# Block sums spread by DMA, a third value buffer, an earlier v load, and two more x tiles transposed by DMA in a sparse-attention and expert-mixture kernel

## The chip, the cores and the metric

The kernel runs on one core of one Trainium2 chip. The metric is device time in microseconds (us). Before the change the median of 6 runs was 668.28 us (667.62 to 671.56).

## The reference

Two stages follow each other. The first is attention over 4 batches of 8 heads, 768 positions and 64 channels. Each query sees the keys less than 16 positions away, and 24 block summaries: the maximum of each block of 32 keys, and the mean of the 32 values. The second sends each of the 3072 rows of x (512 wide) through 8 experts and adds their outputs with weights P, which come from a gate and 8 rounds of row and column normalisation.

```python
k_sum = k.reshape(B, H, nb, block, D).max(axis=3)        # block = 32, nb = 24
v_sum = v.reshape(B, H, nb, block, D).mean(axis=3)
mask_l = np.abs(pos[:, None] - pos[None, :]) < window    # window = 16
scores_s = scale * np.einsum('bhsd,bhnd->bhsn', q, k_sum) + np.log(block)
...                                                      # one softmax over near keys and summaries
x = attn_out.transpose(0, 2, 1, 3).reshape(B * S, H * D)
P = np.exp(logits)                                       # logits = x @ w_gate, less the maximum
for _ in range(8):
    P /= P.sum(1, keepdims=True) + 1e-09
    P /= P.sum(0, keepdims=True) + 1e-09
    P *= N / E
for e in range(E):
    out += P[:, e:e + 1] * (np.maximum(x @ w1[e], 0.0) @ w2[e])
```

## The kernel before, in words

The heads are worked on in 16 pairs (two heads fill the 128 partitions), four pairs to a batch. Pairs 0 to 3 go in halves of 384 positions and have code of their own; the change concerns pairs 4 to 15. For such a pair:

- POOL issues the loads of k, q and v from HBM (`load_qk` L268, `load_v` L285), which are cast to bf16 on the way. k and q are transposed, by TensorE for pairs 4 to 11 (`tr`, L301, tile `tkq`) and by DMA transposes issued on SP for pairs 12 to 15 (`tr_dma`, L328).
- `key_max` takes block maxima of k on VectorE, and `key_max_split` (L339) lays those of the two heads into columns 0 to 63 of `ksT`.
- `block_sums` (L355, tile `vs`) sums v over blocks with 6 matmuls. `block_out` scales the sums into chunk 0 of `V_e` (L361) and copies that chunk to the other five on VectorE (L365). `V_e` holds, for each of the 6 chunks of 128 positions, 64 rows of summaries and 64 rows with the 16 positions next to the chunk on either side. These neighbour rows are copied from v by four small DMAs (`near_values`, L375 and L377), issued on SP for pairs 4 to 11 and on POOL after that. There are NE = 2 buffers of `V_e`.
- `scores` (L345, tile `sg`) multiplies keys and near queries; a head has 64 channels, so these matmuls use 64 rows of the array. ScalarE takes the exponential (L406), and VectorE masks it (L410) and lays the edges out (L418, L422).
- `summaries_2` (L459, tile `ss`) multiplies the block maxima with the queries: two matmuls of 64 columns, one for each half of the positions, into the two halves of the partitions. ScalarE takes the exponential (L470).
- `values` (tile `av`) multiplies weights and values: 6 matmuls on the chunk itself (L433) and 3 with `V_e` (L439), for each half. `normalize` divides (L540, L541).
- `to_xT` transposes the result with 6 matmuls (L548, tile `tx`) and `x_out` copies it out on ScalarE or VectorE; for pairs 12, 13 and 14 a DMA transpose on SP does this (`x_dma`, L558, from X_BY_DMA = 12 on).

Between these units TensorE does expert 0: `hps` (L209, x times w1) and `yps` (L214, hidden times w2), and the gate (`lp`, L568) once for each batch. Experts 1 to 7 follow (L762, L813) with a scheme that saves multiplications by sums formed on VectorE, and with the sums into `out_acc` done by VectorE and by DMAs that add.

The order on every engine is fixed when the program is built. A planner (`Plan.order`) holds units with an engine, a cost, dependences, a priority and a lag, and places the unit that can start first; the costs in `load_pair`, `pair_start` and `pair_whole` decide the order, not the times on the chip. All engines work off their queues in order, so a unit that waits holds up what stands behind it. On POOL stand the loads of a pair, then the next pair's; before batch 1 the order is k and q of pair 4, w2 of expert 0, the constants of two `V_e` buffers (L694 to L697) and two edge buffers (L690), v of pair 4, then pairs 5 and up. On SP stand the neighbour copies of the pairs, and the DMA transposes.

Of the kernel before, what the change touches and what calls it, by code (L numbers as in the profile page):

```python
# [10 lines left out]
BF16 = mybir.dt.bfloat16  # L11
# [117 lines left out]
def kernel(  # L129
# [10 lines left out]
    nc = tc.nc  # L140

    B, H, S, D = q.shape
    G = S // 128
# [6 lines left out]
    NP = (B * H) // 2  # L150
    PB = H // 2
    SCALE = 1.0 / float(D) ** 0.5
    W = 16
# [4 lines left out]
    VD = D + 1  # L158
    NEH = 3
    BY_DMA = 12  # L160
    X_BY_DMA = 12
    WHOLE = 12
    FILL = {"v0": 1, "S0": 1, "s0": 2, "s1": 1, "s2": 1}

# [53 lines left out]
    NQ = 6  # L218
    NB = PB
    NE = 2  # L220
    NS = 1
    NA = 3
    stage = ExitStack()
    with tc.manual_schedule():
# [12 lines left out]
        kT = [attn.tile([128, S], BF16, name=f"kT{i}") for i in range(NB)]  # L237

        ks = [attn.tile([128, 1, 32], BF16, name=f"ks{i}") for i in range(NB)]
        ksT = [attn.tile([128, 128], BF16, name=f"ksT{i}") for i in range(NB)]  # L240
        v_x = [attn.tile([128, 2, G, VD], BF16, name=f"vx{i}") for i in range(NQ)]

        E_h = [attn.tile([128, 2, HG + 1, PADL], BF16, name=f"Eh{i}") for i in range(NEH)]
        V_s = [attn.tile([128, 2 * VD], BF16, name=f"Vs{i}") for i in range(PB)]

        E_e = [attn.tile([128, G, 128], BF16, name=f"Ee{i}") for i in range(NE)]
        V_e = [attn.tile([128, G, 2 * VD], BF16, name=f"Ve{i}") for i in range(NE)]

        BLK = 512
        NPAIR = N // (2 * BLK)  # L250
# [85 lines left out]

        def key_max_split(i):
            r = i % NB
            nc.vector.tensor_tensor(out=ksT[r][:, 0:64].rearrange("p (j n) -> p j n", j=2),  # L339
                                    in0=ks[r][:].to_broadcast([128, 2, 32]),  # L340
                                    in1=own[:].to_broadcast([128, 2, 32]), op=ALU.mult)

# [14 lines left out]

        def block_out(i):
            vs = at.pop(("vs", i))[0:64, :].rearrange("p (j d) -> p j d", j=2)
            dst = V_s[i][0:64, :] if i < PB else V_e[i % NE][0:64, 0, :]  # L360
            nc.vector.tensor_tensor(out=dst.rearrange("p (j x) -> p j x", j=2)[:, :, 0:D], in0=vs,  # L361
                                    in1=own_n[:].to_broadcast([64, 2, D]), op=ALU.mult)
            if i >= PB:
                ve = V_e[i % NE]
                nc.vector.tensor_copy(out=ve[0:64, 1:G, :],  # L365
                                      in_=ve[0:64, 0:1, :].to_broadcast([64, G - 1, 2 * VD]))


        def near_values(i):

            sv, ve = v_x[i % NQ], V_e[i % NE]
            eng = nc.sync if i < BY_DMA else nc.gpsimd
            for j in range(2):
                c0, q0 = VD * j, 64 + 32 * j
                eng.dma_start(out=ve[q0 + W:q0 + 2 * W, 1:G, c0:c0 + VD],  # L375
                              in_=sv[128 - W:128, j, 0:G - 1, :])
                eng.dma_start(out=ve[q0:q0 + W, 0:G - 1, c0:c0 + VD],  # L377
                              in_=sv[0:W, j, 1:G, :])
# [46 lines left out]
                                        op=ALU.mult)  # L425

        def values(i, h):
            sv, ee, ve, em = v_x[i % NQ], E_e[i % NE], V_e[i % NE], at["em", i]
            av = at["av", i, h] = bank("a", "av")
            for cc in range(HG):  # L430
                c, o = HG * h + cc, cc * 2 * VD
                for j in range(2):
                    nc.tensor.matmul(av[:, o + j * VD:o + (j + 1) * VD],  # L433
                                     lhsT=em[:, j, c, :], rhs=sv[:, j, c, :],
                                     start=(cc == 0 and j == 0), stop=False,
                                     skip_group_check=True)
            for cc in range(HG):
                c, o = HG * h + cc, cc * 2 * VD
                nc.tensor.matmul(av[:, o:o + 2 * VD], lhsT=ee[:, c, :], rhs=ve[:, c, :],  # L439
                                 start=False, stop=True, skip_group_check=True)  # L440

        def summaries(i, h, tag):
            r = i % NB
            ss, rhs = bank(tag, "ss"), qT[r][:, W + h * HS:W + (h + 1) * HS]
            wait_busy("s", i, h, ss)
            at["ss", i, h] = ss
            if i < PB and not h:
                for j in range(2):
                    p = slice(64 * j, 64 * j + 64)
                    nc.tensor.matmul(ss[32 * j:32 * j + 32, 0:HS], lhsT=ks[r][p, 0, :], rhs=rhs[p],  # L450
                                     start=True, stop=True)
                return
            nc.tensor.matmul(ss[:, 0:HS], lhsT=ksT[r][:], rhs=rhs, start=True, stop=True)

        def summaries_2(i):
            r, ss = i % NB, bank("a", "ss")
            for h in range(2):
                at["ss", i, h] = ss[64 * h:64 * h + 64]
                nc.tensor.matmul(ss[64 * h:64 * h + 64, 0:HS], lhsT=ksT[r][:, 0:64],  # L459
                                 rhs=qT[r][:, W + h * HS:W + (h + 1) * HS], start=True, stop=True)  # L460

        def summary_exp(i, h):
            if i < PB:
# [187 lines left out]
        def constants():  # L651
# [8 lines left out]
            for t in ks:  # L660
                nc.vector.memset(t[:, 0, 24:32], 0.0)
            for t in ksT:
                nc.vector.memset(t[:, 64:128], 0.0)
# [201 lines left out]
        def load_pair(i, parts="kqv"):  # L865
            old = i - NQ
            for c in parts:
                if c == "v":
                    load(("v", i), lambda: load_v(i), 1.05, 1.85,
                         [U.get(("A", old, 1)), U.get(("near", old))])  # L870
                elif i < PB and c in "qr":
                    h = "qr".index(c)
                    load(("q", i, h), lambda h=h: load_qk(i, 1, h), 0.65, 0.65)
                else:
                    z = "kq".index(c)
                    load((c, i), lambda z=z: load_qk(i, z), 0.75 if i < PB else 1.65,
                         1.2 if i < PB else 1.55, [U.get(("tr", old, z)), U.get(("tr", old, 2))])

        def pair_start(i, prio):
            o = i - NB  # L880
# [20 lines left out]
            U["vs", i] = add("PE", 0.4, lambda: block_sums(i),  # L901
                             [U["v", i]] + ([U.get(("A", i - NE, 1)), U["vc", i % NE]] if i >= PB else []), prio + 0.01, opens=[buf])
            sc = add("DVE", 0.25, lambda: summary_constants(i), [], prio - 1.0) if 0 < i < PB else None
            U["Vs", i] = add("DVE", 0.28 if i < PB else 0.7, lambda: block_out(i), [U["vs", i], sc],
                             prio + 0.01, uses=[buf])

        def pair_half(i, h, prio):
# [33 lines left out]

        def pair_whole(i, prio):
            U["near", i] = add("SP" if i < BY_DMA else "POOL", 2.4 if i < BY_DMA else 3.0, lambda: near_values(i),
                               [U["v", i], U.get(("A", i - NE, 1)), U["vc", i % NE]], prio, lag=3.5)
            x1 = []
            deps = [U["kT", i, 0], U["kT", i, 1], U.get(("ed", i - 2))]
            bufs = [Buffer("s")] + (2 * [None] if i < WHOLE else [Buffer("a"), Buffer("a")])
# [12 lines left out]
            for h in range(2):  # L960
# [5 lines left out]
            U["ss", i, 0] = U["ss", i, 1] = add("PE", 0.22, lambda: summaries_2(i),  # L966
                                                [U["km", i], U["kT", i, 1], U.get(("A", i - NE, 1))], prio, opens=[buf])
# [124 lines left out]
        def transposed():  # L1092
# [6 lines left out]
            ve = V_e[(NP - 1) % NE]  # L1099
# [4 lines left out]
        last[0] = add("POOL", 0.3, transposed, [last[0], U["near", NP - 1]] + [U["kT", NP - 1, z] for z in range(2)]  # L1104
                      + [U["x", i] for i in range(X_BY_DMA, NP - 1)])
        load("w1n", lambda: load_w1(1), 0.85, 5.0)
        load("w2n", lambda: load_w2(1), 0.85, 5.0)
# [209 lines left out]
```

## Time and profile before

| what | value |
|---|---|
| median of 6 runs | 668.28 us (667.62 to 671.56) |
| the profiled execution, its own time | 671.9 us |
| its span, first to last instruction | 670.2 us |
| mean granted TensorE clock | 0.997 |
| packets under 512 B | 77920 of 112542 |
| median time to landing: k, q, v loads | 5.7, 5.5, 6.2 us |
| w (a whole weight), neighbour copies from SP, from POOL | 10.5, 5.2, 2.1 us |
| DMA transposes of k, q, x | 4.8, 4.0, 3.3 us |

The profile is of one execution. Its page gives the busy time of each engine, with TensorE's matmuls as PE and its weight loads as PEld, then the span in 40 slices of 16.8 us in tenths. A matmul's duration is its latency: several overlap, and what one costs the queue is the distance from its start to the start of the next. A wait line reads: engine, tile and line, what it waited for, microseconds in total, how often, the longest. A timeline line reads: start, microseconds, engine, line, operation, output and inputs, the part of the array in rows and columns, shape, how many. A line of the chain that ended last has start, duration and what ran. All lines of code are those of the kernel before.

### The profile page before, as it was taken

The numbers are of one execution on the slowest core, as the hardware profiler recorded it, in microseconds if no ns is written. First come the engines' busy times: TensorE is split into PE (matmuls) and PEld (weight loads), VectorE is DVE, ScalarE is ACT, GpSimd is POOL, SyncE is SP. The second block draws the span as 40 slices with busy tenths as digits, with TensorE's granted clock in tenths as the row PEclk, the third lists the DMA queues.
The fourth block names the chain that finished last, engine by engine and source line by source line (L and its number), as shares of the span: only waits on it lengthen the run. The fifth ranks groups of instructions, "written<-read, shape, count | busy, mean of one in ns | idle before, by whom it ended". The sixth has DMA issues, their size and how long they took to land.

```text
span 670.2 us, 13245 instructions
## 1 busy us (share of the span) xinstructions
PE 660.1 (98%) x5132; PEld 434.8 (65%) x5132; DVE 546.1 (81%) x1027; ACT 415.8 (62%) x776; POOL 198.2 (30%) x256
## 2 busy tenths in 40 slices
PE   9979999999999999999999999999999999999996
PEld 5646665555676666666666666666666666666665
DVE  7859877798989787788779886888778877988776
ACT  6757876565886666656565556656655656556652
POOL 8899522100031221222132222222222113222123
PEclk9989999999999999999999999999999999999999
DMA  9999971610754738374654656473847465334656
GB/s 164 172 144 145 120 97 30 118 21 1 126 95 80 126 62 127 64 128 78 95 95 69 121 86 104 78 126 53 126 76 123 78 100 95 63 63 111 157 134 198
DMA packets 112542, 67.89 MB, mean 101 GB/s; under 512 B 77920, under 2 KB 90464, under 8 KB 112480
## 3 DMA queue, kind: packets, MB, share of 16 engines
q0 software_dynamic: 94800, 57.46, 64.4%
q1 hardware_dynamic: 17152, 9.58, 5.8%
q8 instruction: 40, 0.66, 0.4%
q14 instruction: 22, 0.18, 0.1%
q10 hardware_dynamic: 528, 0.02, 0.0%
HBM read 52.45 MB, written 6.29 MB: 88 GB/s over the span
## 4 chain that ended last, share of the span: by engine, by line
PE 93%; DMA 3%; POOL 2%; SPq 0%; issue 0%; DVE 0%; ACT 0%; POOLq 0%; DVEq 0%
PE yps L813 22%; PE pA L762 22%; PE pY L813 16%; PE pQ L762 11%; PE yps L214 6%; PE hps L209 6%; PE pR L762 5%; DMA w<-in_moe_w_dram 1%; DMA vx<-in_v_dram 1%; DMA Ve<-vx 1%; PE sg L345 1%; PE av L433 1%; PE av L439 1%; PE tkq L301 1%; PE vs L355 1%; PE ss L459 0%
## 5 line engine op out<-in xcount | busy, mean ns | idle before, releaser
L813 PEld LDWEIGHTS <-h 128*128 128x128 f16 x2352 | 229.8, 98 | 89.5 <-issue 1.0
L841 POOL DMA_DIRECT2D out_acc<-y x120 | 101.4, 886 | 372.9 <-ACT y L837 108.8
L837 ACT ACTIVATE y<-pY,P_sb 128x256 f32<-128x256 f32 x168 | 79.9, 476 | 124.1 <-PE pY L813 122.3
L828 DVE SCALAR_TENSOR_TENSOR out_acc<-yps,P_sb,out_acc 128x512 f32<-128x512 f32 x128 | 95.2, 744 | 29.4 <-PE yps L813 29.4
L796 DVE TENSOR_TENSOR h<-h 128x1024 f16<-128x1024 f16 x168 | 109.1, 684 | 1.4
L813 PE MATMUL pY<-w,h 128*128 128x256 f16 x672 | 100.0, 273 | 0.6 <-ACT y L837 0.6
L813 PE MATMUL yps<-w2sum,h 128*128 128x256 f16 x672 | 98.4, 273 | 0.0
L762 PE MATMUL pA<-xT,w 128*128 128x512 f16 x336 | 98.4, 380 | 0.0
L813 PE MATMUL yps<-w,h 128*128 128x256 f16 x672 | 93.2, 273 | 0.0
L828 DVE SCALAR_TENSOR_TENSOR out_acc<-pY,P_sb,out_acc 128x512 f32<-128x512 f32 x84 | 62.9, 748 | 31.6 <-PE pY L813 30.1
L762 PEld LDWEIGHTS <-w 128*128 128x128 f16 x672 | 65.7, 98 | 31.6 <-issue 0.2
L762 PEld LDWEIGHTS <-w1sum 128*128 128x128 f16 x504 | 49.3, 98 | 44.4
L784 DVE CUSTOM_DVE_ANT_0 h<-pQ,snap 128x512 f16<-128x512 f32 x84 | 57.6, 686 | 6.1 <-ACT snap L205 3.6
L784 DVE CUSTOM_DVE_ANT_0 h<-pA,snap 128x512 f16<-128x512 f32 x84 | 57.4, 683 | 5.5 <-PE pA L762 5.2
L200 ACT ACTIVATE h<-pA 128x512 f16<-128x512 f32 x84 | 50.6, 603 | 13.3 <-PE pA L762 13.1
L200 ACT ACTIVATE h<-pR 128x512 f16<-128x512 f32 x84 | 50.1, 596 | 8.6 <-PE pR L762 8.1
L205 ACT COPY pR<-pA 128x512 f32<-128x512 f32 x83 | 47.4, 571 | 6.9 <-PE pA L762 6.0
L813 PE MATMUL pY<-w2sum,h 128*128 128x256 f16 x336 | 50.4, 273 | 0.0
L762 PE MATMUL pQ<-xsum,w1sum 128*128 128x512 f16 x168 | 50.0, 380 | 0.0
L762 PE MATMUL pA<-xsum,w1sum 128*128 128x512 f16 x168 | 50.0, 380 | 0.0
L762 PE MATMUL pQ<-xT,w1sum 128*128 128x512 f16 x168 | 50.0, 379 | 0.0
L762 PE MATMUL pA<-xsum,w 128*128 128x512 f16 x168 | 50.0, 379 | 0.0
(150 smaller groups left out, 854.1 us busy)
## 6 DMA issues: line engine op xcount, KB each, us to landing
out_acc<-y POOLq DMA_DIRECT2D x120, 256.0 KB, 3.4
w<-in_moe_w_dram POOLq DMA_DIRECT2D x15, 1024.0 KB, 10.5
out_dram<-out_acc SPq DMA_DIRECT2D x24, 256.0 KB, 2.4
qst<-in_q_dram POOLq DMA_DIRECT2D x32, 96.0 KB, 5.5
vx<-in_v_dram POOLq DMA_DIRECT2D x15, 192.0 KB, 6.2
kst<-in_k_dram POOLq DMA_DIRECT2D x24, 96.0 KB, 5.7
w<-in_moe_w_dram POOLq DMA_DIRECT2D x4, 256.0 KB, 7.4
kst<-in_k_dram POOLq DMA_DIRECT2D x3, 192.0 KB, 4.5
```

The costliest lines, as they stand in the source:

```text
L200: nc.scalar.activation(out=out, in_=in_, func=AF.Relu, bias=0.0, scale=1.0)
L205: (nc.scalar.copy if eng == "ACT" else nc.vector.tensor_copy)(out=out, in_=in_)
L209: nc.tensor.matmul(hp[:, 0:n], lhsT=w1s[e][:, dk, f * 128:(f + 1) * 128], rhs=xT[:, dk, t0:t0 + n], start=(dk == 0), stop=(dk == KD - 1))
L214: nc.tensor.matmul(yp[:, d], lhsT=h[:, f, c * 128:(c + 1) * 128], rhs=w2s[e][:, f, d], start=(f == 0), stop=(f == KF - 1))
L301: nc.tensor.transpose(t[:, g * 128:(g + 1) * 128], st[:, g, :, :].rearrange("p j d -> p (j d)"), ident)
L762: nc.tensor.matmul(dst[:], lhsT=lhsT, rhs=rhs, start=first and k == 0, stop=k == HK - 1, skip_group_check=True)
L784: nc.vector._custom_dve(dve_ops.TENSOR_ADD_SAT, out=ring(e, p, q)[:, q % 2, blk, :], in0=at[src, e, p, q][:], in1=at.pop(("snap", n, e, p, ...
L796: nc.vector.tensor_tensor(out=h[:, :, out_, :], in0=h[:, :, a, :], in1=h[:, :, b, :], op=op)
L813: nc.tensor.matmul(dst[:, d], lhsT=lhsT, rhs=rhs, start=f == 0 and n in (1, 5, 2), stop=f == HF - 1, skip_group_check=True)
L828: nc.vector.scalar_tensor_tensor(out=o, in0=y, scalar=scalar, in1=o, op0=ALU.mult, op1=ALU.add)
L837: nc.scalar.activation(out=at[key][:, d], in_=src, func=AF.Copy, bias=0.0, scale=P_sb[:, t, e:e + 1])
L841: nc.gpsimd.dma_start(out=o, in_=at.pop(("y", e, p, c, key))[:], accum_op=ALU.add)
```

## The change

- The copy of the block sums to chunks 1 to 5 leaves VectorE. `spread_sums` does it with one DMA that reads chunk 0 five times; it is issued on SP for pairs 4 to 11 and on POOL for 12 to 15, and the values of the pair wait for it.
- `V_e` gets three buffers (NV = 3), with one more set of constants on POOL.
- v of pair 4 is loaded ahead of w2 of expert 0.
- The planner's costs of loads and its lags of the DMAs on SP are changed, and so the order on all engines.
- `ksT` becomes 192 columns wide, zeros on both sides of the keys. The two summary matmuls then take 128 columns each and add into the same bank: the first has the keys in its first 64 columns, the second in its last.
- X_BY_DMA goes from 12 to 9: the results of pairs 9 and 10 are transposed by DMA too (pair 11 is not, as pair 15 is not).

```diff
-    X_BY_DMA = 12
+    X_BY_DMA = 9
...
+    NV = 3
...
-        ksT = [attn.tile([128, 128], BF16, name=f"ksT{i}") for i in range(NB)]
+        ksT = [attn.tile([128, 192], BF16, name=f"ksT{i}") for i in range(NB)]
...
-        V_e = [attn.tile([128, G, 2 * VD], BF16, name=f"Ve{i}") for i in range(NE)]
+        V_e = [attn.tile([128, G, 2 * VD], BF16, name=f"Ve{i}") for i in range(NV)]
...
-            if i >= PB:
-                ve = V_e[i % NE]
-                nc.vector.tensor_copy(out=ve[0:64, 1:G, :],
-                                      in_=ve[0:64, 0:1, :].to_broadcast([64, G - 1, 2 * VD]))
...
+        def spread_sums(i):
+
+            ve = V_e[i % NV]
+            (nc.sync if i < BY_DMA else nc.gpsimd).dma_start(
+                out=ve[0:64, 1:G, :], in_=ve[0:64, 0:1, :].to_broadcast([64, G - 1, 2 * VD]))
...
-                nc.tensor.matmul(ss[64 * h:64 * h + 64, 0:HS], lhsT=ksT[r][:, 0:64],
-                                 rhs=qT[r][:, W + h * HS:W + (h + 1) * HS], start=True, stop=True)
+                nc.tensor.matmul(ss[:, 0:HS], lhsT=ksT[r][:, 64 - 64 * h:192 - 64 * h],
+                                 rhs=qT[r][:, W + h * HS:W + (h + 1) * HS], start=h == 0, stop=h == 1)
...
-                    load(("v", i), lambda: load_v(i), 1.05, 1.85,
+                    load(("v", i), lambda: load_v(i), 1.05, 1.85 if i < PB else 1.6,
...
-                         1.2 if i < PB else 1.55, [U.get(("tr", old, z)), U.get(("tr", old, 2))])
+                         1.2 if i < PB else 1.4, [U.get(("tr", old, z)), U.get(("tr", old, 2))])
...
-                               [U["v", i], U.get(("A", i - NE, 1)), U["vc", i % NE]], prio, lag=3.5)
+                               [U["v", i], U.get(("A", i - NV, 1)), U["vc", i % NV]], prio, lag=5.0 if i < BY_DMA else 3.5)
+            U["sp", i] = add("SP" if i < BY_DMA else "POOL", 0.62 if i < BY_DMA else 0.9, lambda: spread_sums(i), [U["Vs", i]],
+                             prio, lag=5.0 if i < BY_DMA else 3.5)
...
-                                   [U["mk", i, h], U["ed", i], U["sx", i, h], U["Vs", i], U["near", i]],
+                                   [U["mk", i, h], U["ed", i], U["sx", i, h], U["sp", i], U["near", i]],
...
-        load_pair(PB, "kq")
-        load("w2", lambda: load_w2(0), 0.85, 5.0)
+        load_pair(PB, "kqv")
+        load("w2", lambda: load_w2(0), 0.85, 4.0)
+        for n in range(NV):
+            U["vc", n] = last[0] = add("POOL", 1.2, lambda n=n: value_constants(n), [last[0]])
         for n in range(NE):
-            U["vc", n] = last[0] = add("POOL", 1.2, lambda n=n: value_constants(n), [last[0]])
             U["ec", n] = last[0] = add("POOL", 0.7, lambda n=n: edge_constants(n), [last[0]])
...
-            load_pair(i, "v" if i == PB else "kqv")
+            load_pair(i, "" if i == PB else "kqv")
```

More of the change, by code (lines that the diff above doesn't have):

```diff
@@ L338, in key_max_split @@
             r = i % NB
-            nc.vector.tensor_tensor(out=ksT[r][:, 0:64].rearrange("p (j n) -> p j n", j=2),
+            nc.vector.tensor_tensor(out=ksT[r][:, 64:128].rearrange("p (j n) -> p j n", j=2),
                                     in0=ks[r][:].to_broadcast([128, 2, 32]),
@@ L359, in block_out @@
             vs = at.pop(("vs", i))[0:64, :].rearrange("p (j d) -> p j d", j=2)
-            dst = V_s[i][0:64, :] if i < PB else V_e[i % NE][0:64, 0, :]
+            dst = V_s[i][0:64, :] if i < PB else V_e[i % NV][0:64, 0, :]
             nc.vector.tensor_tensor(out=dst.rearrange("p (j x) -> p j x", j=2)[:, :, 0:D], in0=vs,
                                     in1=own_n[:].to_broadcast([64, 2, D]), op=ALU.mult)
-            if i >= PB:
-                ve = V_e[i % NE]
-                nc.vector.tensor_copy(out=ve[0:64, 1:G, :],
-                                      in_=ve[0:64, 0:1, :].to_broadcast([64, G - 1, 2 * VD]))
+        def spread_sums(i):
+            ve = V_e[i % NV]
+            (nc.sync if i < BY_DMA else nc.gpsimd).dma_start(
+                out=ve[0:64, 1:G, :], in_=ve[0:64, 0:1, :].to_broadcast([64, G - 1, 2 * VD]))
         def near_values(i):
-            sv, ve = v_x[i % NQ], V_e[i % NE]
+            sv, ve = v_x[i % NQ], V_e[i % NV]
             eng = nc.sync if i < BY_DMA else nc.gpsimd
@@ L427, in values @@
         def values(i, h):
-            sv, ee, ve, em = v_x[i % NQ], E_e[i % NE], V_e[i % NE], at["em", i]
+            sv, ee, ve, em = v_x[i % NQ], E_e[i % NE], V_e[i % NV], at["em", i]
             av = at["av", i, h] = bank("a", "av")
@@ L452, in summaries @@
                 return
-            nc.tensor.matmul(ss[:, 0:HS], lhsT=ksT[r][:], rhs=rhs, start=True, stop=True)
+            nc.tensor.matmul(ss[:, 0:HS], lhsT=ksT[r][:, 64:192], rhs=rhs, start=True, stop=True)
         def summaries_2(i):
@@ L662, in constants @@
             for t in ksT:
-                nc.vector.memset(t[:, 64:128], 0.0)
+                nc.vector.memset(t[:], 0.0)
             for t, n in ((own, 64), (own_n, 32)):
@@ L901, in pair_start @@
             U["vs", i] = add("PE", 0.4, lambda: block_sums(i),
-                             [U["v", i]] + ([U.get(("A", i - NE, 1)), U["vc", i % NE]] if i >= PB else []), prio + 0.01, opens=[buf])
+                             [U["v", i]] + ([U.get(("A", i - NV, 1)), U["vc", i % NV]] if i >= PB else []), prio + 0.01, opens=[buf])
             sc = add("DVE", 0.25, lambda: summary_constants(i), [], prio - 1.0) if 0 < i < PB else None
-            U["Vs", i] = add("DVE", 0.28 if i < PB else 0.7, lambda: block_out(i), [U["vs", i], sc],
+            U["Vs", i] = add("DVE", 0.28, lambda: block_out(i), [U["vs", i], sc],
                              prio + 0.01, uses=[buf])
@@ L965, in pair_whole @@
             buf = Buffer("a")
-            U["ss", i, 0] = U["ss", i, 1] = add("PE", 0.22, lambda: summaries_2(i),
+            U["ss", i, 0] = U["ss", i, 1] = add("PE", 0.33, lambda: summaries_2(i),
                                                 [U["km", i], U["kT", i, 1], U.get(("A", i - NE, 1))], prio, opens=[buf])
@@ L1098, in transposed @@
                 nc.gpsimd.tensor_copy(out=warm[:, 4:5], in_=xT[0:32, PB - 2, (B - 1) * S:(B - 1) * S + 1])
-            ve = V_e[(NP - 1) % NE]
+            ve = V_e[(NP - 1) % NV]
             for j in range(2):
@@ L1102, in transposed @@
                                       in_=ve[64 + 32 * j:96 + 32 * j, G - 2, VD * j:VD * j + 1])
-        last[0] = add("POOL", 0.3, transposed, [last[0], U["near", NP - 1]] + [U["kT", NP - 1, z] for z in range(2)]
+        last[0] = add("POOL", 0.3, transposed, [last[0], U["near", NP - 1], U["sp", NP - 1]] + [U["kT", NP - 1, z] for z in range(2)]
                       + [U["x", i] for i in range(X_BY_DMA, NP - 1)])
```

## The prediction

> **What bounds the kernel now.** I read the page first, then who waited for whom on TensorE over the whole span, then the chain that ended last around the one wait found there, the stretches in tens of microseconds, and last TensorE's timeline. The page:
>
> ```profile
> span 670.2 us, 13245 instructions
> ## 1 busy us (share of the span) xinstructions
> PE 660.1 (98%) x5132; PEld 434.8 (65%) x5132; DVE 546.1 (81%) x1027; ACT 415.8 (62%) x776; POOL 198.2 (30%) x256
> ...
> PEclk9989999999999999999999999999999999999999
> ```
>
> TensorE (PE) is busy 98% of the span, and one slice of its clock (the third, 33 to 50 us) is not full. The waits of TensorE over the whole span:
>
> ```profile
> PE av L439 <- DMA Ve<-vx: 3.5, 1, 3.5
> PE idle L611 <- DVE zeros L630: 1.3, 1, 1.3
> PE pY L813 <- ACT y L837: 0.6, 1, 0.6
> ```
>
> Everything after that one wait is TensorE-bound: what TensorE saves or loses in attention moves the end by as much, and work taken off VectorE is worth nothing in itself. The wait belongs to pair 4, the first pair of batch 1; the chain leads to it:
>
> ```profile
> 22.94 0.88 POOL w L196
> ...
> 27.88 7.01 DMA vx<-in_v_dram
> ...
> 34.98 0.76 SPq L375
> ...
> 35.80 1.44 SPq L377
> ...
> 37.92 6.59 DMA Ve<-vx
> ```
>
> v of pair 4 is issued at 27.88 behind w2 (22.94), lands at 34.89, the fourth neighbour copy goes out at 37.92 and lands at 44.51; TensorE stood from 41.1. The stretches show what follows (columns: PE busy, clock, DMA share, GB/s):
>
> ```profile
> 30.00:40.00 10.00, 10.00 (x138) 1.00 2.17 155
> 40.00:50.00 10.00, 6.46 (x61) 0.83 2.21 140
> 50.00:60.00 10.00, 10.00 (x117) 1.00 2.32 145
> ```
>
> The granted clock was 0.83 there: 0.17 x 10 = 1.7 us more. The stall costs 3.5 + 1.7 = **5.2 us** of this execution.
>
> **The change, part by part.**
>
> *v of pair 4 ahead of w2.* Its load is issued at about 22.9, five microseconds earlier, so it lands near 29 and the neighbour copies (2.5 to 3.5 us of issue on SP, 4.5 median and 6.7 at most to landing in the rows of Ve) near 38 to 39. The changed order puts TensorE at that pair's values at about 41.0: its block sums stand where w2's first matmul stood (32.80), and between them and L439's successor are 20 yps at 0.216, 24 lp at 0.025, 27 transposes and block-sum matmuls at 0.056, 2 summary matmuls at 0.163, one score group 0.40, the values of pair 3 0.84 and 6 av at 0.03: 8.2 us. So the 5.2 us go. Next late is w2. TensorE's timeline shows it was just in time:
>
> ```profile
> 32.43 0.51 PE L548 MATMUL tx<-ident_x,xs 128*128 128x128 f16 x6
> 32.80 1.02 PE L214 MATMUL yps<-w,h 128*128 128x512 f16 x4
> ```
>
> w2 is issued at 22.91 and its row has 9.8 us to landing: 32.76, against a start at 32.80. One v load ahead of it in the same saturated queue (DMA share above 2 in the stretches) costs between 1.3 (the steady distance from a q landing to the v landing behind it) and 2.1 (v of pair 4 behind w2). The block sums moved ahead give 0.34 back. TensorE then waits 1.0 to 1.7 for w2; I take 1.2. The nearest row for what an idle of that length does to the clock is the 3.5 us stall (-1.7 more); a third as long, I take nothing, and keep 1.7 as the end. In the Trainium skill, "TensorE: Matmul & The Clock Gate" (Part 1) puts the fall to half rate after an idle window of about 3.4 us; the 3.5 us row agrees, and by the page this wait would cost no clock.
>
> *Loads behind it.* The changed order also brings block sums forward: those of pair 9 now stand 21.9 us of TensorE work behind those of pair 4 (32 hps at 0.163, 24 yps, 24 lp, 81 short ones at 0.056, 54 av, 6 score groups, 6 summary matmuls, pair 3's values), at 54.7, plus the w2 wait: 55.9. In the trace before v of pair 9 is issued at 50.44; with the row's 6.2 us it lands at 56.6, which harmed nobody, because its block sums ran at 71.04. The third buffer's constants put 1.33 us more (23.86 to 25.19 is one set) on POOL ahead of these loads, which POOL issues without a break (4.25 us a pair). So v of pair 9 lands at 56.6 to 58.0 and TensorE waits 0.7 to 2.1 more, partly already at pairs 6 and 7; I take 1.0.
>
> *Spread by DMA.* Removes 12 VectorE copies of 0.483 = 5.8 us; no wait of TensorE named VectorE after 48 us, so this is worth 0. Added: 12 issues of about 0.6 on SP or 0.52 on POOL, and a landing of 1.7 to 6.7 us where the copy was done in 0.5. What hides it is the distance from a pair's block sums to its values: for pair 4 8.2 us plus the w2 wait against 0.3 + 0.6 + 4.5 to 6.7, more for later pairs (pair 5: 9.8). Cost 0; a latency beyond 9 us would uncover it, one for one, first at pair 4. Its bytes: 64 x 5 pieces of 260 B, as many pieces as the four neighbour copies together. By pieces that is 320 / 1536 of a v load's 1.3 us, 0.3 of the saturated queue a pair; the other end is a whole v load, 1.3. I take 0.3, the nearest in pieces and size, inside the 1.0 above. The wait on SP stands ahead of the next pair's neighbour copies, whose v lands later anyway.
>
> *Three value buffers* free neighbour copies one pair earlier; those waited on SP, no TensorE wait named them after pair 4: 0.
>
> *Full-width summary scores.* The rows, all at full clock:
>
> ```profile
> 92.92 0.34 PE L439 MATMUL av<-Ve,Ee 128*128 128x130 bf16 x3
> 93.10 0.34 PE L433 MATMUL av<-vx,em 128*128 128x65 bf16 x6
> 93.28 0.34 PE L439 MATMUL av<-Ve,Ee 128*128 128x130 bf16 x3
> 93.54 0.35 PE L459 MATMUL ss<-qT,ksT 128*64 128x384 bf16 x2
> 93.83 1.47 PE L209 MATMUL hps<-xT,w 128*128 128x384 f16 x8
> 95.14 0.51 PE L355 MATMUL vs<-vx,m_blk 128*128 128x128 bf16 x6
> ```
>
> Three av matmuls take 0.18 to the next full-width one but 0.26 to the summary pair, the pair 0.29 until the next starts: 0.37, of which two halves side by side need only 0.16. Full width costs twice 0.164 (hps x8: 1.31) = 0.33 and no change of shape. Eight of the 12 pairs stand behind full-width work and cost 0.37, four behind scores and cost 0.29 (the scores' own way out is paid either way): 4.1 us before, 12 x 0.33 = 3.9 after: **-0.2**. The Trainium skill speaks against this edit: "TensorEngine Tiling (Array Packing)", Theoretical Speedup, gives half-wide tiles up to twice the rate, by which full width would add 12 x 0.16 = 1.9 us; its Key Properties say too that a change of mode drains the engine, and the row of 93.54 prices that above the gain.
>
> *x of pairs 9 and 10 by DMA.* Removes 12 transposes at 0.056 = **-0.7** from TensorE, and two copies (0.8 ScalarE or 0.56 VectorE), off the path. Adds two transposes on SP (1.21 of issue, 3.3 to landing). Behind each on SP's queue stand transposes of k and q for pairs 13 to 15, which in the trace were issued 10 us and more ahead of use. Cost 0; uncovered, one for one.
>
> Sum on this execution: 671.9 - 5.2 - 0.7 - 0.2 + 1.2 + 1.0 = 668.0, a gain of 3.9. Profiled, it took 3.6 more than the median of 668.28. From 48 us on TensorE is full either way, so most of these 3.6 must lie in the loads before it: part of the stall or its slow clock is probably missing from the runs timed, and then part of the new waits too. The gain on the median lies between 1.4 (the stall worth 1.6, new waits 1.1) and 3.9; I take 2.5: **665.8**.
>
> **Rivals.**
> 1. *Nothing new waits*, w2 and the v loads landing sooner than in this execution: 668.28 - 2.5 - 2.2 = 663.6. For it: the median below the profile. Against: w2's margin of 0.04 us.
> 2. *The stall only moves*: the queue sets the pace, and w2 and the v loads cost what the neighbour copies cost. What stays is 0.9 for the matmuls: 667.4. For it: DMA share above 2 until 76 us.
> 3. *Slower*: the spread's 260-byte pieces slow the loads to 5.5 us a pair (4.2 + 1.3). v of pair 5, issued at 32.12 and landed at 39.7, then comes at 41.0, v of pair 9 at 41.0 + 4 x 5.5 = 63.0, 8.3 behind TensorE's 54.7, with one stretch long enough for the clock (1.7): 10.0 against 6.1 taken away, 3.9 slower, 672.2. It decides from a pace of 4.5 (with the slow clock) to 5.0 (without). Against: those pieces take a fifth of a load's number.
> 4. *The change doesn't do what it says*: pair 4 still waits, on its spread in place of its neighbours. That needs 9 us of latency; the longest row is 6.7. Counted in 3.
>
> **How the numbers follow.** Forecast 0.48 at 665.8 (a fifth of it within 0.3% of the median), nothing new waits 0.18, stall only moves 0.23, slower 0.11. About 0.3%, 2.0 us, is what a measurement of this kernel tells from no change: faster 0.48 x 0.8 + 0.18 = 0.56, same 0.33, slower 0.11. The range runs from 663.0 (rival 1 with the loads' lower ends) to 669.5, leaving out most of rival 3 and a little at the bottom.
>
> **What would show it.** Right: no wait at the values of pair 4, a clock of 1.00 from 40 to 50 us; a wait of about 1.2 us of the first yps for w2; small waits of block sums for v at pairs 6 to 9; summary matmuls 128 x 128, 0.33 a pair; attention ending 3 to 5 us earlier in the trace. Wrong: the clock falling again, values waiting for Ve from Ve, block sums waiting over 3 us, or a wait after 130 us, where I expect TensorE to stay full.

## The result, and the profile after

The change made the kernel slower: 672.93 us median of 24 runs (670.63 to 675.89) against 668.84 of 48 runs of the kernel before beside them (666.57 to 673.74), a ratio of 1.0061 with a 95% interval of 1.0047 to 1.0074. The forecast was 665.8, the range 663.0 to 669.5. The profiled execution took 672.14 us; its sum in the prediction was 668.0. Lines of code named for the kernel after are one higher than before's from L222 on, and three higher behind the spread.

First the page of the kernel after and the waits of TensorE over the whole span (microseconds in total, times, the longest):

```profile
span 670.1 us, 13260 instructions
PE 657.7 (98%) x5120; PEld 434.1 (65%) x5120; DVE 545.9 (81%) x1022; ACT 409.3 (61%) x767; POOL 201.9 (30%) x264
...
PEclk9999999999999999999999999999999999999999
```
```profile
PE sg L346 <- DVE qT L205: 3.3, 1, 3.3
PE vs L356 <- DMA vx<-in_v_dram: 2.2, 3, 1.1
PE idle L614 <- DVE zeros L633: 1.3, 1, 1.3
PE pY L816 <- ACT y L840: 0.6, 1, 0.6
```

The wait at the values of pair 4 is gone, and the clock is full in every slice of this execution. In that it is not typical: of the 24 executions, 22 had a mean granted clock of 0.994 to 0.997, the profiled one is one of the two at 1.00. Of 138 executions of before, timed beside the experiments, 54 had a mean clock under 0.998. And a wait of 3.3 us for VectorE stands where there was none, and block sums (`vs`) wait three times for v. The stretches show where TensorE stands (PE busy, clock, DMA share, GB/s); the second fence is the kernel before:

```profile
40.00:50.00 10.00, 9.34 (x123) 1.00 2.20 153
50.00:60.00 10.00, 8.87 (x116) 1.00 2.27 159
70.00:80.00 10.00, 10.00 (x127) 1.00 2.05 137
80.00:90.00 10.00, 6.54 (x67) 1.00 2.00 141
90.00:100.00 10.00, 10.00 (x101) 1.00 1.23 130
```
```profile
70.00:80.00 10.00, 10.00 (x139) 1.00 1.77 117
80.00:90.00 10.00, 10.00 (x106) 1.00 1.64 136
90.00:100.00 10.00, 10.00 (x109) 1.00 0.37 68
```

From 80 to 100 us the DMA engines carried 2.00 and 1.23 where they had carried 1.64 and 0.37: the loads end later, and more of the DMA transposes now run beside them. In before, the first two transposes of k (issued at 77.27 and 80.23, beside loads) took 7.2 and 6.1 us, the two after them 2.9 and 3.5. What that did to TensorE is read in two steps. VectorE's timeline of the kernel after (in brackets the idle time before, and its releaser):

```profile
83.65 0.95 DVE L334 TENSOR_REDUCE ks<-kT 128x24 bf16<-128x768 bf16 x1 [4.47 <-DMA kT<-kst]
84.52 0.55 DVE L205 COPY kT<-tkq 128x768 bf16<-128x768 bf16 x1
84.98 0.55 DVE L205 COPY qT<-tkq 128x768 bf16<-128x768 bf16 x1
```

The first line is `key_max` of pair 12; behind it stand the copies of pair 11's transposed k and q. TensorE's scores of pair 11 need these copies; its transposes for them had begun at 79.75 and 80.08, and VectorE stood idle from 79.18, so the copies could have run some 4 us earlier. The chain that ended last shows what `key_max` waited for:

```profile
74.53 9.10 DMA kT<-kst
83.63 0.02 issue
83.65 0.95 DVE ks L334
84.60 0.46 DVE kT L205
85.07 0.47 DVE qT L205
```

The DMA transpose of k of pair 12 took 9.10 us. It was also issued late: k had landed at 68.26, but on SP's queue the neighbour copies and the spread of pair 11 (71.08 to 74.35) stood ahead of it. The DMA rows (KB each, median us to landing) tell that the long transpose is no single accident; before, k took 4.8 and q 4.0:

```profile
vx<-in_v_dram POOLq DMA_DIRECT2D x15, 192.0 KB, 6.9
...
Ve<-Ve SPq DMA_DIRECT2D x8, 81.2 KB, 5.8
...
kT<-kst SPq DMA_TRANSPOSE x4, 8.6
qT<-qst SPq DMA_TRANSPOSE x4, 8.5
```

### The profile page after: what moved, and what is told of

The parts are those of the page before. It is cut to its first block, busy times and chain, and to the rows that moved or that the text cites. A ratio compares the mean times of both kernels' runs of the same rounds, so it can differ in the third digit from the quotient of the medians.

```text
span 670.1 us, 13260 instructions
## 1 busy us (share of the span) xinstructions
PE 657.7 (98%) x5120; PEld 434.1 (65%) x5120; DVE 545.9 (81%) x1022; ACT 409.3 (61%) x767; POOL 201.9 (30%) x264
## 3 DMA queue, kind: packets, MB, share of 16 engines
q0 software_dynamic: 94992, 57.79, 64.3%
q1 hardware_dynamic: 21440, 10.64, 7.9%
## 4 chain that ended last, share of the span: by engine, by line
PE 89%; POOL 5%; DMA 4%; DVE 1%; issue 1%; ACT 0%; POOLq 0%; DVEq 0%
PE yps L816 22%; PE pA L765 22%; PE pY L816 16%; PE pQ L765 11%; PE pR L765 5%; PE yps L214 5%; PE hps L209 4%; DMA kT<-kst 1%; DMA w<-in_moe_w_dram 1%; POOL vx L288 1%; POOL qst L283 1%; POOL kst L283 1%; DMA vx<-in_v_dram 1%; PE sg L346 1%; PE ss L462 0%
## 5 line engine op out<-in xcount | busy, mean ns | idle before, releaser
L205 ACT COPY pR<-pA 128x512 f32<-128x512 f32 x80 | 45.6, 570 | 8.9 <-PE pA L765 7.7
L765 PE MATMUL pR<-xT,w 128*128 128x512 f16 x168 | 50.0, 379 | 0.0
## 6 DMA issues: line engine op xcount, KB each, us to landing
Ve<-Ve SPq DMA_DIRECT2D x8, 81.2 KB, 5.8
```

Source lines behind the costliest of these rows:

```text
L205: (nc.scalar.copy if eng == "ACT" else nc.vector.tensor_copy)(out=out, in_=in_)
L765: nc.tensor.matmul(dst[:], lhsT=lhsT, rhs=rhs, start=first and k == 0, stop=k == HK - 1, skip_group_check=True)
```

## The experiments

Two theories stood against each other. **A, place in the queue:** the planner gave the transpose of k too short a lag, so `key_max` of pair 12 came to stand ahead of pair 11's copies on VectorE; put it behind them and the loss goes. **B, traffic:** the spread's small pieces slow what shares the DMA engines, and the wait shows up wherever a load or transpose is late. A third, **C**, was that the x transposes on SP hold up those of k and q. The order in which the planner puts the units changes with almost every edit, so an edit below is priced together with its order unless the text says that the order was held. In the times below, the kernel before measured 668.35 to 669.32 beside each group of runs; ratios are to it.

**Queue place alone undone.** After, with one dependence more:

```diff
-            U["ks", i] = add(..., [U["kT", i, 0], U.get(("km", o))], prio)
+            U["ks", i] = add(..., [U["kT", i, 0], U.get(("km", o))]
+                             + ([U["kT", i - 1, z] for z in range(2)] if i == BY_DMA else []), prio)
```

> The changed kernel with one dependence more in the planner: VectorE's block maxima of pair 12 (they need k of pair 12, transposed by DMA) come after its copies of pair 11's transposed k and q. Theory A (place in VectorE's queue): the 3.3 us wait of pair 11's scores, and in most runs the half-rate clock after it, are gone; 672.9 falls by 3.3 to 5.0, to 668 to 669.6. Rival B (traffic: spread and x transposes fill the DMA engines): k of pair 12 still lands 9 us after its issue, the wait turns up again at the summary scores or values of pairs 10 to 12; 671.5 to 673.

Measured 672.0 (670.21 to 673.31), ratio 1.0042 [1.0023, 1.0062]. TensorE's waits, then VectorE's line behind the first of them:

```profile
PE vs L356 <- DVE xs L544: 3.0, 1, 3.0
PE vs L356 <- DMA vx<-in_v_dram: 2.9, 3, 1.9
```
```profile
92.77 0.95 DVE L334 TENSOR_REDUCE ks<-kT 128x24 bf16<-128x768 bf16 x1 [4.05 <-DMA kT<-kst]
```

The wait at pair 11's scores went and came back one pair later, at 94.93, in the same form: `key_max` of pair 13 waits for its transposed k. A falls as the whole cause, as far as pair 12's place on VectorE goes. Not tested alone: an order in which no `key_max` stands ahead of ready copies, and the place of pair 12's transposes on SP.

**x by TensorE again.** After, with `X_BY_DMA = 12`.

> The changed kernel with X_BY_DMA back at 12: x of pairs 9 and 10 transposed by TensorE. VectorE's maxima of pair 12 still stand ahead of pair 11's copies. Theory A: the wait of pair 11's scores stays (k of pair 12 is issued ahead of the x transposes anyway), and 12 transposes at 0.056 come back: 672.9 to 674. Rival C (the x transposes delay k of pair 12): it lands 7 us after issue as before the change, the wait shrinks to 1.5 or less: 669.5 to 671.

Measured 674.41 (672.75 to 675.59), ratio 1.0074 [1.0046, 1.0101]. The wait at pair 11's scores stayed (3.7 us) and k of pair 12 took 9.90 us with no x transpose ahead of it. C falls for that wait.

**Spread by VectorE again.** After, with the copy on VectorE:

```diff
-            (nc.sync if i < BY_DMA else nc.gpsimd).dma_start(
-                out=ve[0:64, 1:G, :], in_=ve[0:64, 0:1, :].to_broadcast([64, G - 1, 2 * VD]))
+            nc.vector.tensor_copy(out=ve[0:64, 1:G, :],
+                                  in_=ve[0:64, 0:1, :].to_broadcast([64, G - 1, 2 * VD]))
...
-            U["sp", i] = add("SP" if i < BY_DMA else "POOL", ...)
+            U["sp", i] = add("DVE", 0.45, lambda: spread_sums(i), [U["Vs", i]], prio + 0.01)
```

> The changed kernel with the block sums copied by VectorE again (three buffers and the earlier v load stay). The planner then also puts the maxima of pair 12 behind pair 11's copies. Theory A: no wait at pair 11's scores, for the order alone; 668 to 669. Rival B: besides, the waits of block sums for v (2.2 us in the changed kernel) fall below 1 us and k of pair 12 lands in 7 us or less after issue: 666 to 667.5.

Measured 669.44 (668.25 to 671.28), ratio 1.0003 [0.9981, 1.0025]: 3.5 us of the loss went with the spread by DMA. The block sums no longer wait. One wait is left in attention:

```profile
PE lp L571 <- DMA xT<-xs: 2.7, 1, 2.7
```

It is x of pair 10, issued at 84.87 and landed 8.67 us later: here the x transposes do cost something. The transposes of k and q took nearly as long as in after, with no spread by DMA in the kernel:

```profile
kT<-kst SPq DMA_TRANSPOSE x4, 8.3
qT<-qst SPq DMA_TRANSPOSE x4, 8.2
```

So transposes of 8 us come without the spread's DMA too. But here SP issued pair 12's ahead of pair 11's neighbour copies (k at 65.94, landed 5.9 us later), `key_max` of pair 12 stood behind pair 11's copies, and VectorE waited for none of them. The planner's order had changed, so this run alone doesn't tell traffic from order.

**The earlier v load alone.** Before, with the load of v of pair 4 ahead of w2 and nothing else.

```diff
-        load_pair(PB, "kq")
+        load_pair(PB, "kqv")
...
-            load_pair(i, "v" if i == PB else "kqv")
+            load_pair(i, "" if i == PB else "kqv")
```

> The kernel before with v of pair 4 loaded ahead of w2 and nothing else. The wait of pair 4's values for its neighbour copies (3.5 us and a half-rate clock in the profiled execution) goes. If the median of before holds a stall of 1.6 us or more, 668.8 falls by 1.5 to 3, to 666 to 667.3; if the runs timed hardly have it, or w2 then lands over 1 us late, it stays within 1 us of 668.8. A clock of 1.00 in both.

Measured 667.58 (667.32 to 671.8), ratio 0.9976 [0.9955, 0.9996]: the gain that the prediction looked for is there, 1.3 us below 668.84. In 11 of its 12 executions the mean clock was 0.998 or more; of before's 29 beside it, in 17.

**Traffic with the order held.** VectorE spreads, as in the run of 669.44, and the spread's DMA is issued as well, into a part of `out_acc` that is written only later; TensorE's and VectorE's orders are those of that run.

```diff
+        def idle_spread(i):
+            d = out_acc[0:64, NT - 1 - i % NV, 0:(G - 1) * VD].bitcast(BF16).rearrange("p (c x) -> p c x", c=G - 1)
+            (nc.sync if i < BY_DMA else nc.gpsimd).dma_start(
+                out=d, in_=V_e[i % NV][0:64, 0:1, :].to_broadcast([64, G - 1, 2 * VD]))
```

> VectorE spreads the sums, as in the run before that gave 669.4, and the spread's DMA is issued as well, at the place that the change gives it on SP and POOL, into a piece of memory that nobody reads yet: the values do not wait for it, and TensorE's and VectorE's orders are those of the run of 669.4. Theory A (order and dependence): the cost of the spread by DMA is the order that the planner makes of it and the wait of the values, so this stays at 669.4 (668.5 to 670.3) and the transposes of k and q land as they did there. Theory B (traffic): the 320 pieces of 260 B a pair and their issue on SP slow what shares the DMA engines, so this goes to 671 to 673, transposes of k and q for pairs 12 and 13 landing 8 us or more after their issue, with waits of block sums for v and of scores for k or q.

Measured 672.14 (670.63 to 675.94), ratio 1.0048 [1.0023, 1.0074], though nobody waits for this DMA. B holds in its time. Its sign, transposes of 8 us or more (8.2 and 8.4 in the median here), tells little, as they took 8.3 and 8.2 without this DMA; only k of pair 12 took clearly longer, 8.6 against 5.9. The longest waits of TensorE in attention:

```profile
PE lp L576 <- DMA xT<-xs: 2.9, 1, 2.9
PE vs L356 <- DMA vx<-in_v_dram: 1.2, 1, 1.2
```

The wait for x was there before (2.7); the wait of block sums for v, at 52.37, is new. In this execution the clock fell behind the wait for x (0.83 from 90 to 100 us; the row is in the last section), in the profiled one of 669.44 it did not.

**Issue or pieces.** The same with one partition in place of 64: 5 pieces a pair, issue and wait on SP whole.

> The run of 672.1 (VectorE spreads, the spread's DMA issued as well and read by nobody, three buffers) with that DMA cut to one partition: 5 pieces of 260 B a pair in place of 320, the orders of all compute engines the same. If the traffic is the cost: 669.4, as without it (668.5 to 670.3). If the issues and waits on SP's queue are: 672. Half of each: 670.5 to 671.

Measured 669.09 (666.56 to 670.51), ratio 1.0003 [0.9984, 1.0023]; its slowest run is faster than the fastest with 320 pieces. So the issues and waits on SP cost nothing that can be seen, and the pieces 3.0 us. About half of that goes with the clock: 11 of the 12 executions with 320 pieces had a mean clock of 0.997 or less, 1 of the 12 with 5 pieces and 5 of the 12 without this DMA. A fall costs 1.7 us in the rows shown, so ten more of twelve are 1.4 us by an estimate. The DMA rows, first with 5 pieces, then with 320:

```profile
q1 hardware_dynamic: 18832, 9.98, 6.5%
...
vx<-in_v_dram POOLq DMA_DIRECT2D x15, 192.0 KB, 5.7
```
```profile
q1 hardware_dynamic: 21440, 10.64, 7.3%
...
vx<-in_v_dram POOLq DMA_DIRECT2D x15, 192.0 KB, 6.8
```

The load of v, on another queue, lands 1.1 us later in the median; the three other runs of the new planner costs without these pieces on SP, with 5.4 to 5.8, agree. From pair 5 to pair 12 its landings are 4.09 us apart with 5 pieces (39.15 to 67.77) and 4.52 with 320 (38.39 to 70.01). Here the three others lie between, at 4.36 to 4.48, with v of pair 12 landing at 68.28 to 69.19.

An earlier pair of runs had tried the same on before with v first and x by DMA, which has two buffers: 667.27 (666.52 to 668.54) with 5 pieces, 669.85 (667.61 to 675.0) with 320. There the idle DMA's read also held the buffer (VectorE waited 2.7 us for it once), so the 2.6 us between them are not traffic alone.

> Before with v of pair 4 ahead of w2 and with x of pairs 9 and 10 transposed by DMA (666.7 by itself), and with a spread's DMA on SP and POOL that nobody waits for, cut to one partition: 5 pieces of 260 B a pair in place of 320. The wait on SP for VectorE's block sums and the issue are whole, the traffic is gone; TensorE's and VectorE's orders are those of the run of 666.7. If the issue and the wait on SP's queue cost the time: as with all 320 pieces, 668.5 to 670. If it is the traffic: 666.7 (666.2 to 667.5).

> The same with all 64 partitions: 320 pieces a pair. Theory B (traffic and issue together) goes by the 2.7 us that the idle spread cost in the run of 672.1 against 669.4: 669.4 (668.3 to 670.5), with a wait over 1 us in attention. If that cost came from the new planner costs and the third buffer, with which that run had little room: 666.7 to 667.5, and no such wait.

**Pieces or bytes.** The idle spread with 320 pieces of 32 B (16 columns of 130).

> The run of 672.1 (VectorE spreads; the spread's DMA is issued as well and read by nobody), its 320 pieces a pair kept, but each of 32 B in place of 260 B; the orders of all engines are the same. If the number of pieces is the cost: 672 (671 to 673), with the load of v at a median of 6.8 us to landing as there. If the bytes are: one eighth of 3.0 us above the 669.1 of the run with 5 pieces, 669.5, and the load of v at 5.7.

Measured 670.29 (667.42 to 672.22), ratio 1.0008 [0.9982, 1.0033]: between the two, and not settled. Its executions fall into two groups: four with a full clock (median 668.11) and eight with 0.997 (671.08). The row of SP's queue is the same as with 260 B (7.3%), that of v is 5.9.

**Which pairs.** The idle spread for pairs 12 to 15 on POOL alone.

```diff
+            if i >= BY_DMA:
+                add("POOL", 0.9, lambda: idle_spread(i), [U["Vs", i]], prio)
```

> The run of 672.1 with the idle spread left to pairs 12 to 15 alone, issued on POOL; the eight on SP (pairs 4 to 11) are gone. If the cost comes from the eight that run beside the loads (v landing later from pair to pair): 669.1 to 669.8. If it comes in proportion to the pairs, four of twelve: 670.1. If the late four, beside the transposes of k and q, are it: 672.

Measured 669.51 (667.18 to 670.49), ratio 1.0000 [0.9977, 1.0023]: the late four are not the cost. 670.1, a cost in proportion to the pairs, lies inside the interval, so this run favours the eight on SP but doesn't prove them the whole of it.

**Neither spread nor x by DMA.** The run of 669.44 with `X_BY_DMA = 12`: v first, three buffers, full width and the new costs stay.

> The change without its spread by DMA and without the x transposes of pairs 9 and 10 by DMA: v of pair 4 ahead of w2, three value buffers, full-width summary scores and the planner's new costs stay. If the wait of 2.7 us for x of pair 10 in the run without the spread was the price of the x transposes, it goes and 12 transposes of 0.056 come back: 669.4 - 2.7 + 0.7 = 667.4 (666.5 to 668.3), and no wait over 0.5 us in attention. Rival: the planner's new order or the third buffer costs something too; then it stays at 668.5 to 670.

Measured 668.84 (667.59 to 671.63), ratio 1.0001 [0.9979, 1.0022]. The wait for x is gone, but the time is the rival's; 667.4 lies outside the interval.

**Full width alone.** Before with v first and the full-width scores, with the change's planner cost of 0.33.

> Before with v of pair 4 ahead of w2 (667.6 by itself) and with the full-width summary scores. Theory of the prediction (two half-width matmuls side by side cost 0.37 with their change of shape, two full-width ones 0.33): 667.6 - 0.2 = 667.4 (666.6 to 668.2). Rival (half-wide tiles run side by side for half the time, the change of shape costs nothing): 12 x 0.16 = 1.9 more, 669.5.

Measured 668.36 (667.17 to 671.79), ratio 0.9991 [0.9971, 1.0012], 0.8 above v first alone.

**x by DMA alone.** Before with v first and `X_BY_DMA = 9`.

> Before with v of pair 4 ahead of w2 (667.6 by itself) and with x of pairs 9 and 10 transposed by DMA. Theory of the prediction (nothing waits for these transposes): 12 x 0.056 saved, 666.9 (666.0 to 667.7). Rival: on SP's queue and in the DMA engines they stand in the way of the transposes of k and q, or land late beside the loads, as in the run without the spread; a wait of 1 to 3 us, 668 to 670.

Measured 666.68 (666.38 to 667.62), ratio 0.9959 [0.9940, 0.9979]: the best of all runs, faster than both kernels. Its longest waits of TensorE in attention:

```profile
PE hps L209 <- DMA w<-in_moe_w_dram: 0.5, 1, 0.5
PE vs L355 <- DMA vx<-in_v_dram: 0.4, 1, 0.4
```

**x by DMA and full width.**

> Before with v of pair 4 ahead of w2, x of pairs 9 and 10 by DMA (666.7 by itself) and full-width summary scores. Theory of the prediction: 666.7 - 0.2 = 666.5. If full width costs what it seemed to cost when it was alone (668.4 against 667.6): 667.5. If half-wide tiles ran side by side for nothing: 668.6.

Measured 669.21 (668.36 to 672.81), ratio 1.0019 [0.9997, 1.0041]; a wait of 2.0 us for neighbour copies had come in with another order of TensorE and VectorE. So the same once more with the planner's cost left at 0.22, which leaves every engine's order as in the run of 666.68:

```diff
-            U["ss", i, 0] = U["ss", i, 1] = add("PE", 0.33, lambda: summaries_2(i),
+            U["ss", i, 0] = U["ss", i, 1] = add("PE", 0.22, lambda: summaries_2(i),
```

> Before with v of pair 4 ahead of w2, x of pairs 9 and 10 by DMA and full-width summary scores, the planner's cost of the scores left at 0.22, so that every engine has the order of the run of 666.7 (in the run of 669.2 the cost of 0.33 had changed TensorE's and VectorE's orders). Theory of the prediction (a pair of half-width matmuls costs 0.37 or 0.29 with its changes of shape, a full-width pair 0.33): 666.7 - 0.2 = 666.5 (666.1 to 667.0). Half-wide tiles for half the time: 668.6. If full width itself costs what the run of 669.2 showed: 669.

Measured 667.06 (666.35 to 668.37), ratio 0.9980 [0.9961, 0.9999]. Full width by itself is worth nothing that can be seen; the 2.1 us between the two runs are the order that a cost of 0.11 more made.

## Why the prediction was wrong

The runs make a ladder of medians from before to after:

| step | median, us | difference |
|---|---|---|
| before | 668.84 | |
| v of pair 4 ahead of w2 | 667.58 | -1.3 |
| full-width scores, with the cost of 0.33 | 668.36 | +0.8 |
| three buffers, the planner's other costs | 668.84 | +0.5 |
| x of pairs 9 and 10 by DMA | 669.44 | +0.6 |
| the spread's issue, 5 pieces a pair | 669.09 | -0.4 |
| its 320 pieces a pair | 672.14 | +3.0 |
| values wait for it, VectorE's copy gone | 672.93 | +0.8 |

The rows come from several groups of runs, beside which before's median lay between 668.35 and 669.32. The steps under 1 us lie inside that scatter; the first just leaves it, and the 3.0 of the 320 pieces is clear of it.

The prediction's sum can be put beside the profiled execution of after. What it took away was right there, what it added was not: TensorE's waits in attention came to 6.0 us (0.1 for w2, 2.2 for v, 3.3 at pair 11's scores, 0.4 in small ones) where the sum has 2.2. With 6.0, 671.9 - 5.2 - 0.7 - 0.2 + 6.0 = 671.8, against 672.14 measured.

*The stall at pair 4.* Right in mechanism: it went, and with v first alone the clock fall in 11 of 12 executions. The prediction took 5.2 us for it on the profiled execution and 1.4 to 3.9 net on the median; alone it gave 1.3. The profiled execution of before, 671.9, was among its longer ones, with a clock fall that 54 of 138 executions show; the prediction suspected as much.

*w2's wait.* 1.2 forecast; w2 landed at 33.24, its first matmul began at 33.28, and it cost 0.1. In the other traces of after's planner costs it was nothing in four, 0.1, 0.2, 1.1 and 2.0, so the forecast lay inside the spread but above most.

*Loads behind it.* 0.7 to 2.1 forecast with 1.0 taken, up to pair 9; 2.2 measured at pairs 5, 6 and 9 (0.41, 0.66 and 1.14).

*Spread by DMA: the step that failed.* "I take 0.3, the nearest in pieces and size, inside the 1.0 above" and "Cost 0; a latency beyond 9 us would uncover it". The latency was fine, 5.8 us, and no values waited for it. The traffic was mis-sized: 0.3 us, hidden inside the 1.0, against 3.0 us measured with the order held (672.14 against 669.09). A pair's share of the engines was about as forecast. The row of SP's queue grew from 6.5 to 6.9% in four runs of the new planner costs without the 320 pieces to 7.3%, so by 0.4 to 0.8% of 16 engines' 670 us, which is 0.3 to 0.7 for each of eight pairs. But the prediction took the delay once. In the loads' queue it adds up: v of pair 12 landed 0.8 to 2.2 us later than in the traces without the pieces on SP (70.01 against 67.77 to 69.19). In the held order this was paid by the block sums (1.3 us of waits for v, where the runs of 669.44 and 669.09 have none) and by the clock, to which the sum gave nothing (1.4 us by the estimate above). Rival 3 had the adding up, with 1.3 a pair. Its time, 672.2, came close by luck: it has v of pair 9 at 63.0, which landed at 57.55.

The 3.3 us wait at pair 11's scores in after is not explained by the pieces alone. The run of 672.14 has the pieces and, in the median, transposes about as long, but not this wait; after has it with pair 12's transposes put behind pair 11's neighbour copies on SP and with `key_max` of pair 12 ahead of the copies of pair 11's k and q on VectorE. No run holds after's own order and takes the pieces away.

In the Trainium skill, "DMA: Bandwidth & Descriptors" (Why small descriptors are slow) holds that copies from SBUF to SBUF don't pay for small descriptors. The 3.0 us of the 260 B pieces speak against taking that as free: beside the loads, others pay for them, whether for their number or their bytes. The page's fit for a DMA issued by POOL (Anatomy of one DMA — SWDGE (gpsimd) path: 2.0 us and bytes over 436 GB/s) would give an estimate of 2.2 us for one spread of 81.2 KB; the four on POOL took 4.7 in the median, the eight on SP 5.8.

*"x of pairs 9 and 10 by DMA ... Cost 0".* The gain was right with before's planner costs and v first: 0.9 measured against 0.7, with a changed order and inside the scatter. In the change's order it went with 0.6 more, and a wait of 2.7 us for x of pair 10. The margin of "10 us and more" was read from before, where the transpose of k of pair 12 was issued at 77.27 and landed at 84.43, and VectorE waited for none of them. In after it was issued at 74.53, VectorE wanted it at 79.18, and it landed at 83.63.

*VectorE "worth 0".* No run speaks against this for the work taken off it. It left out that VectorE works off its queue in order: with `key_max` of pair 12 put ahead of copies that were ready, a late DMA on one side became a wait of TensorE on the other. None of the signs in the prediction named a wait of that kind; "block sums waiting over 3 us" was the nearest.

*Full-width scores.* Forecast -0.2; with the order held, 667.06 against 666.68, no difference. In after's timeline the pair costs 0.34 (88.14 to 88.48), as forecast. The rule of the Trainium skill weighed there ("TensorEngine Tiling (Array Packing)", Theoretical Speedup) would by the prediction's estimate have made it 1.9 slower, to 668.6; the runs don't show that. What a run with it lost, 2.1 us, came through the planner.

What stays open: what of the 3.0 us is the number of pieces and what the bytes; fewer and longer pieces were not tried. What after's order on SP and VectorE cost without the pieces was not run either. And the small steps of the ladder, 0.5 to 0.8 each, go with changes of the order and were not taken apart.

## What to carry to other kernels

An operation moved from an engine with room to the DMA queues isn't free because nobody waits for it: count its pieces against the loads that share the engines, add the delay up over all the iterations that are issued without a break, and ask what the waits it makes do to the clock, over all executions and not in the profiled one alone. An in-order engine turns a late transfer for a later tile into a wait for an earlier one, so read the changed order of every engine for a waiting instruction put ahead of ready ones. Before you blame traffic for a slow transfer, see how long the same transfer takes in a run without that traffic. A planner's changed cost is a change of its own: hold the order when an edit is to be priced.

## What the hardware showed that was not expected

**The clock after short waits.** The prediction let a wait of 1.2 us cost no clock, by the 3.5 us stall as the nearest row. In after's row of 80 to 90 us, shown above, a wait of 3.3 us left the clock at 1.00. Two rows with shorter waits, of the run that spreads 5 pieces a pair (2.0 us, for w2) and of the one with the idle spread (2.9, for x), in the same columns:

```profile
30.00:40.00 10.00, 7.96 (x92) 0.83 1.90 147
```
```profile
90.00:100.00 10.00, 7.11 (x75) 0.83 0.96 111
```

Each lost 1.7 us of full clock, as much as the 3.5 us stall of before. The run with the queue place undone kept 1.00 through a wait of 3.0 us. So the length of a wait alone doesn't tell what it does to the clock. One execution doesn't tell either: 22 of 24 of after had a lower mean clock, though the profiled one did not. The Trainium skill ("TensorE: Matmul & The Clock Gate", Part 1) has a window of about 3.4 us that runs freely, by which waits of one length can fall differently; that 2.0 us can be enough is less than the whole idle window that it names.

**Pieces on the two queues.** Against the run without it, the idle spread adds 336 packets a pair to the row of SP's queue (21440 less 18752, by eight pairs), but only 48 a pair to the other row (94992 less 94800, by four), where POOL issues the same copy. And the share that the row of SP's queue takes didn't change between 32 B and 260 B a piece: 7.3% for both, against 6.5 to 6.9% without these pieces on SP.
